# A gated-recurrence plus MLP kernel: new start order, decay rows on ScalarE's DMA ring, and q/k turned by the transposing DMA

## The chip, the cores and the metric

The kernel runs on 1 core of one Trainium2 chip. The metric is the device time of one execution in microseconds (us). The kernel before takes 344.27 us (median of 3 runs, 342.91 to 344.88). The span of a profile is about 2 us below the device time of the same run.

Engines: PE is TensorE's matmul side, PEld its weight loads, DVE is VectorE, ACT is ScalarE, POOL is GpSimd, SP is SyncE. A name with q at the end (ACTq, SPq) is that engine's sequencer, issuing a DMA. An engine's ring is the queue through which the DMAs that it issues go. A DMA has landed when its data is written; times to landing are counted from the start of its issue.

## The reference

```python
# attention, per batch and head, D = 48, S = 768; 4 batches, 8 heads
scale = min(|a|, 0.999) / (|a| + 1e-6);  a_n = a * scale        # a = a_re + i a_im
S_t = a_n[t, :, None] * S_{t-1} + k[t, :, None] * v[t, None, :]    # complex state 48 x 48
y[t] = q[t] @ Re(S_t)
# MLP on x = y, as 3072 tokens of 384, hidden 1536
h = gelu(x @ w_gate) * (x @ w_val)
out = x + sigmoid(x @ w_res) * (h @ w_out)
```

## The kernel before

The recurrence is done in chunks. A group `g` is 256 time steps of one batch (2 chunks of 128, three groups to a batch, 12 groups). Two groups are a unit; there are 6 units. A unit has a gating part and an attention part, and its tokens then go through the MLP:

- Gating: logarithm and angle of `a`, cumulative sums over time by a matmul with a triangular matrix, then Exp (`E`, `Ei`) and Sin (`CS`). All of it ends in products `Q` and `K` with 96 columns a head.
- Attention: each head's Q and K are turned (transposed), `at` = KT x QT, masked to `atm`, times `v`, plus the carried state `Gb`; `dk` updates the state.
- MLP: 12 steps of gate (`gp`) and value (`vp`) matmuls, 6 matmuls a step, then `op`.

The program alternates a gating phase (`phase_x`) and an MLP phase (`phase_y`). In the MLP phase of unit u, the first half of the attention of unit u+1 is woven between the gate/value matmuls; in the following gating phase the rest of it. In the trace ScalarE loads another function table (1.28 us each) at each change of phase, which marks the phases.

A group that is not the first of its batch (groups 1, 2, 4, 5, ...) needs its decay factors with the head dimension on the partitions. The kernel writes rows of 384 numbers to DRAM and reads them back turned:

```python
def turn(nm, g, srcs):                       # called for lm (m1), then for E and Ei (m2)
    md = dr.tile([n, DM], FP, ...)           # a scratch in DRAM
    for i, src in enumerate(srcs):
        nc.gpsimd.dma_start(out=md[i:i + 1, :], in_=src)
    m = mp.tile([128, n, H], FP, ...)
    for u in range(2):                       # 4-byte pieces
        nc.gpsimd.dma_start(out=m[u * D:(u + 1) * D]..., in_=md.rearrange("r (h d) -> d (r h)", h=H))
```

Q and K are turned by TensorE, four heads at a time, with a copy out of PSUM:

```python
def a():
    tp = psT.tile([128, 1024], BF, ...)
    ... # 4 nc.tensor.transpose of Q, 4 of K
    qk = sqp.tile([128, 1024], BF, ...)
    nc.scalar.copy(out=qk[0:DD, 0:512], in_=tp[0:DD, 0:512])
    nc.vector.tensor_copy(out=qk[0:DD, 512:1024], in_=tp[0:DD, 512:1024])
    ... # 4 matmuls at = K^T x Q^T, then atm = at * mask
...
def hi(f):                                   # each attention step is recorded like this
    with tc.high_priority():                 # the scheduler puts it as early as its inputs allow
        f()
```

## Time and profile before

The busy shares of the kernel before, in 40 slices of its 341.4 us (each digit is a tenth; PEclk is the granted clock of TensorE):

```profile
PE 267.3 (78%) x2054; PEld 160.6 (47%) x2080; DVE 245.4 (72%) x440; ACT 203.0 (59%) x338; POOL 67.1 (20%) x104
...
PE   0330544298689979899897999779999989999995
...
PEclk9996585559699999999999999999999999999999
DMA  9999999999999999527422620021000210002002
```

DMA is full in the first 16 slices (137 us). In the first 8 (68 us) TensorE is at most half busy; from slice 12 on (94 us) it is nearly full and at full clock.

The chain of work that ended last, within those first 95 us of the kernel before (start us, us, what):

```profile
21.80 6.91 DMA dm_219<-ar
...
44.80 13.88 DMA dm_266<-ar
...
76.31 8.40 DMA dm_663<-Ei
...
85.89 4.42 DMA m_666<-dm_663
```

These are decay rows of 1.5 KB, and their turned copies. So in this chain the start is held mostly by tiny transfers on a full DMA: with two more turned copies of 5.6 and 4.6 us they make up 44 of the 94 us, and the longest piece for an input, a load of `v`, is 8.4 us.

The table of phases used from here on is read from ScalarE's timeline: "start" ends where the gelu table of unit 0 is loaded, an MLP phase goes from a gelu table to the next log/exp table (the last one, which has no following unit, from gelu table to gelu table), a gating phase from there to the next gelu table, and "tail" is the rest of the span. Phases are read to 0.1 us, so that sums can be off by 0.1.

| kernel before | us |
|---|---|
| start | 94.0 |
| five MLP phases | 26.0, 26.4, 26.6, 25.5, 26.0: sum 130.5 |
| four gating phases | 20.8, 20.1, 20.7, 18.5: sum 80.1 |
| tail | 36.9 |

Busy time in the MLP phases of the kernel before, by windows (window, length, busy of PE, PEld, DVE, ACT, POOL with the number of instructions, granted clock, DMA share, GB/s; the sum is over all five. A DMA packet counts in the window in which it starts, so a share can exceed 1):

```profile
187.20:213.80 26.60, 26.05 (x269) 16.75 (x271) 24.31 (x44) 16.79 (x31) 0.00 (x0) 1.00 0.28 53
...
sum 130.50, PE 127.12 PEld 80.69 DVE 116.13 ACT 82.42 POOL 9.01; mean PE 25.42 PEld 16.14 DVE 23.23 ACT 16.48 POOL 1.80
```

TensorE is busy in 127.1 of 130.5 us, VectorE in 116.1.

### The profile page before, as it was taken

What the parts mean: (1) busy time and instruction counts of PE and PEld (TensorE: products, weight loads), DVE (VectorE), ACT (ScalarE), POOL (GpSimd) and SP (SyncE); (2) the same over time, 40 slices, a digit from 0 to 9 for tenths busy, and PEclk for the clock granted to TensorE, in tenths of its full rate; (3) what the DMA queues carried; (4) which work ended last, traced back from release to release, by engine and by line L of the source; (5) the groups of instructions that cost most, each with busy time, mean ns of one, the idle gap of its engine ahead of it and who ended that gap; (6) DMA issues with size and microseconds to landing.
All of it is one profiled execution on the core that took longest, in us unless ns stands there. A gap on an engine that the chain in (4) does not pass through costs nothing.

```text
span 341.4 us, 5552 instructions
## 1 busy us (share of the span) xinstructions
PE 267.3 (78%) x2054; PEld 160.6 (47%) x2080; DVE 245.4 (72%) x440; ACT 203.0 (59%) x338; POOL 67.1 (20%) x104
## 2 busy tenths in 40 slices
PE   0330544298689979899897999779999989999995
PEld 0110224275256545465554566445665556565452
DVE  1322696249999649999389998499994799855443
ACT  3365434349665696756896656977568275662530
POOL 9423710050522224102232000150001300000000
PEclk9996585559699999999999999999999999999999
DMA  9999999999999999527422620021000210002002
GB/s 139 136 139 175 176 184 196 175 170 171 155 167 162 169 133 172 109 46 72 25 63 54 118 46 2 2 48 47 3 2 1 50 46 2 0 2 92 2 1 92
DMA packets 135258, 30.25 MB, mean 89 GB/s; under 512 B 127168, under 2 KB 135232, under 8 KB 135232
## 3 DMA queue, kind: packets, MB, share of 16 engines
q1 hardware_dynamic: 103296, 23.60, 40.6%
q0 software_dynamic: 31936, 6.31, 21.9%
q8 instruction: 16, 0.26, 0.3%
q14 instruction: 10, 0.08, 0.1%
HBM read 31.33 MB, written 4.76 MB: 106 GB/s over the span
## 4 chain that ended last, share of the span: by engine, by line
PE 47%; DMA 18%; DVE 15%; ACT 9%; issue 7%; POOL 3%; ACTq 0%; DVEq 0%; POOLq 0%
PE vp L414 12%; PE gp L410 11%; PE op L434 6%; DMA dm_266<-ar 4%; DMA v<-in_v_dram 4%; PE tp L320 3%; PE at L327 3%; PE tp L317 3%; PE rp L426 3%; DMA dm_663<-Ei 2%; ACT L445 2%; DVE fg L237 2%; DVE r L234 2%; DMA dm_219<-ar 2%; ACT CS L119 2%
## 5 line engine op out<-in xcount | busy, mean ns | idle before, releaser
L410 PE MATMUL gp<-xT,wg 128*128 128x512 bf16 x196 | 61.5, 382 | 7.6 <-DVE xT L401 4.6
L414 PE MATMUL vp<-xT,wv 128*128 128x512 bf16 x210 | 60.3, 382 | 0.3
L322 ACT COPY qk<-tp 96x512 bf16<-96x512 bf16 x48 | 27.9, 581 | 28.3 <-PE tp L320 15.1
L180 DVE TENSOR_TENSOR ai<-s,ai 128x768 f32<-128x768 f32 x12 | 11.1, 955 | 38.5 <-ACT s L119 26.9
L330 DVE TENSOR_TENSOR atm<-at,mask_81 128x512 bf16<-128x512 f32 x48 | 32.8, 683 | 7.2 <-PE at L327 7.2
L410 PEld LDWEIGHTS <-wg 128*128 128x128 bf16 x216 | 20.0, 98 | 23.0 <-issue 8.9
L317 PE MATMUL tp<-ident,Q 128*96 128x128 bf16 x192 | 20.1, 231 | 13.4 <-DVE qk L323 8.6
L142 POOL DMA_DIRECT2D v<-in_v_dram x24 | 21.3, 902 | 43.0 <-PE y L367 22.4
L414 PEld LDWEIGHTS <-wv 128*128 128x128 bf16 x216 | 20.4, 98 | 19.3 <-issue 0.8
L317 PEld LDWEIGHTS <-Q 128*96 128x96 bf16 x192 | 17.3, 131 | 21.4 <-issue 10.0
L323 DVE COPY qk<-tp 96x512 bf16<-96x512 bf16 x48 | 19.9, 414 | 10.1 <-ACT qk L322 9.6
L203 PE MATMUL csl<-ar,lt0a 128*128 128x384 f32 x24 | 12.3, 601 | 18.6 <-DVE ar L189 18.5
L119 ACT ACTIVATE CS<-fg,hpi 128x768 bf16<-128x768 f32 x12 | 11.2, 935 | 24.1 <-DVE fg L237 24.1
L445 ACT ACT_TABLE_LOAD x18 | 23.1, 1283 | 1.0 <-PEq L547 0.7
L320 PE MATMUL tp<-ident,K 128*96 128x128 bf16 x192 | 22.1, 235 | 0.0
L227 PE MATMUL cst<-ai,lt0b 128*128 128x384 f32 x24 | 11.6, 568 | 13.4 <-ACT ai L119 13.1
L327 PE MATMUL at<-qk 96*128 96x128 bf16 x192 | 20.4, 228 | 0.1
L437 DVE SCALAR_TENSOR_TENSOR ot<-sg,op 128x384 f32<-128x384 f32 x24 | 13.2, 549 | 9.4 <-PE op L434 9.4
L365 PE MATMUL y<-v,atm 128*128 128x48 bf16 x192 | 17.9, 187 | 2.5 <-DVE atm L330 2.4
L365 PEld LDWEIGHTS <-atm 128*128 128x128 bf16 x192 | 13.5, 98 | 12.8 <-DVE atm L330 11.6
L320 PEld LDWEIGHTS <-K 128*96 128x96 bf16 x192 | 17.3, 133 | 0.0
L357 PEld LDWEIGHTS <-K 128*96 128x96 bf16 x160 | 13.3, 138 | 6.5 <-DVE K L292 4.2
(155 smaller groups left out, 626.3 us busy)
## 6 DMA issues: line engine op xcount, KB each, us to landing
ar<-in_a_re_dram SPq DMA_DIRECT2D x24, 192.0 KB, 5.7
ai<-in_a_im_dram SPq DMA_DIRECT2D x24, 192.0 KB, 5.5
q<-in_q_dram SPq DMA_DIRECT2D x24, 192.0 KB, 5.1
k<-in_k_dram SPq DMA_DIRECT2D x24, 192.0 KB, 5.0
out_dram<-ot SPq DMA_DIRECT2D x24, 192.0 KB, 1.9
v<-in_v_dram POOLq DMA_DIRECT2D x24, 96.0 KB, 6.3
wg<-in_moe_w_gate_dram POOLq DMA_DIRECT2D x4, 288.0 KB, 9.2
wv<-in_moe_w_val_dram POOLq DMA_DIRECT2D x4, 288.0 KB, 10.5
```

The costliest lines, as they stand in the source:

```text
L142: nc.gpsimd.dma_start(out=t[:, c], in_=rows(v, g, c))
L317: nc.tensor.transpose(out=tp[0:DD, j * 128:j * 128 + 128], in_=Q(x), identity=ident)
L320: nc.tensor.transpose(out=tp[0:DD, 512 + j * 128:640 + j * 128], in_=K(x), identity=ident)
L322: nc.scalar.copy(out=qk[0:DD, 0:512], in_=tp[0:DD, 0:512])
L323: nc.vector.tensor_copy(out=qk[0:DD, 512:1024], in_=tp[0:DD, 512:1024])
L327: nc.tensor.matmul(out=at[:, j], lhsT=qk[0:DD, 512 + j * 128:640 + j * 128], rhs=qk[0:DD, j * 128:j * 128 + 128], start=True, stop=True)
L330: nc.vector.tensor_tensor(out=atm, in0=at, in1=mask4, op=OP.mult)
L365: nc.tensor.matmul(out=ys, lhsT=st["atm", hg][:, j], rhs=V(h), start=True, stop=first)
L410: nc.tensor.matmul(out=gp, lhsT=wg[:, fi, ffi * 128:(ffi + 1) * 128], rhs=xT[:, fi, :], start=(fi == 0), stop=(fi == KD - 1))
L414: nc.tensor.matmul(out=vp, lhsT=wv[:, fi, ffi * 128:(ffi + 1) * 128], rhs=xT[:, fi, :], start=(fi == 0), stop=(fi == KD - 1))
L434: nc.tensor.matmul(out=ps, lhsT=h2[:, ffi, jj * 128:(jj + 1) * 128], rhs=wo[:, ffi, :], start=(ffi == 0), stop=(ffi == KF - 1))
L445: tab(nc.scalar.preload_act_table_set(nm))
```

## The change

The intent: (1) start unit 0 sooner, by loading its inputs first and gating it alone; (2) take the decay rows off GpSimd's ring, where they stand behind weight loads, and put them on ScalarE's; (3) take the Q/K transposes of units 1 to 5 from TensorE, and their PSUM copies from ScalarE and VectorE, and let SyncE's transposing DMA do them; (4) issue the stores on GpSimd. The diff, cut to its core:

```diff
+    PE_TURNED = 2
-    lda bufs=6, ldq bufs=4
+    lda bufs=5, ldq bufs=3;  pF bufs=1 (for fg alone);  pT bufs=3 (for QT and KT)
-    psT = ... bufs=1 ...;  psA = ... bufs=1
+    psA = ... bufs=2
...
+    def decay_rows(g):
+        er = pS.tile([1, DM], FP, tag="r", name="er")
+        act(out=er, in_=T["lm", g][0:1, 0:DM], func=AF.Exp)
+        md = dr.tile([3, DM], FP, tag="md", name="md")
+        for i, src in enumerate((T["E", g - 1][127:128, DM:W], T["Ei", g][0:1, 0:DM], er)):
+            nc.scalar.dma_start(out=md[i:i + 1, :], in_=src)
+    def decay(g):
+        m = mp.tile([128, 3, H], FP, tag="m", name="m")
+        for u in range(2):
+            nc.scalar.dma_start(out=m[u * D:(u + 1) * D]..., in_=T["md", g]...)
+        ... # M = product of the three rows, on GpSimd (was VectorE)
...
     # products: Q and K are written into 128 columns a head, the last 32 zero
+                if g >= PE_TURNED:
+                    for c in range(C):
+                        tt = pT.tile([128, H, 128], BF, tag=nm + "T", name=nm + "T")
+                        nc.sync.dma_start_transpose(out=tt, in_=t[:, c * H:(c + 1) * H]...)
...
-        nc.sync.dma_start(out=out[t0:t0 + 128, :], in_=ot)
+        nc.gpsimd.dma_start(out=out[t0:t0 + 128, :], in_=ot)
...
-    for g in gs(0) + gs(1):
-        load_a(g)
-    for g in gs(0):
-        load_q(g)                     # q, k and v
-    after_landing(T["k", 0], load_w_in)
+    for g in gs(0):
+        load_a(g)
+    for g in gs(0):
+        load_q(g); load_v(g)
+    for g in gs(1):
+        load_a(g)
+    after_landing(T["ai", 2], load_w_in)
+    for g in gs(1):
+        load_q(g)
     # phase_x(-1) gates unit 0 alone; phase_x(0) gates unit 1 and starts unit 2
+            after_landing(T["q", 2], lambda: [load_v(g) for g in gs(1)])
+            after_landing(T["q", 3], load_w_out)
```

More of the change, by code (lines that the diff above doesn't have):

```diff
@@ L85 @@
     wr = singles.tile([128, KD, DM], BF, name="wr")
-    lda = ctx.enter_context(tc.tile_pool(name="lda", bufs=6))
-    ldq = ctx.enter_context(tc.tile_pool(name="ldq", bufs=4))
+    lda = ctx.enter_context(tc.tile_pool(name="lda", bufs=5))
+    ldq = ctx.enter_context(tc.tile_pool(name="ldq", bufs=3))
     ldv = ctx.enter_context(tc.tile_pool(name="ldv", bufs=6))
@@ L92 @@
     pE = ctx.enter_context(tc.tile_pool(name="pE", bufs=2))
+    pF = ctx.enter_context(tc.tile_pool(name="pF", bufs=1))
     pQ = ctx.enter_context(tc.tile_pool(name="pQ", bufs=2))
     pK = ctx.enter_context(tc.tile_pool(name="pK", bufs=1))
+    pT = ctx.enter_context(tc.tile_pool(name="pT", bufs=3))
     sqp = ctx.enter_context(tc.tile_pool(name="sqp", bufs=2))
@@ L103 @@
     psM = ctx.enter_context(tc.tile_pool(name="psM", bufs=4, space=PSUM))
-    psT = ctx.enter_context(tc.tile_pool(name="psT", bufs=1, space=PSUM))
-    psA = ctx.enter_context(tc.tile_pool(name="psA", bufs=1, space=PSUM))
+    psA = ctx.enter_context(tc.tile_pool(name="psA", bufs=2, space=PSUM))
     psY = ctx.enter_context(tc.tile_pool(name="psY", bufs=1, space=PSUM))
     psD = ctx.enter_context(tc.tile_pool(name="psD", bufs=1, space=PSUM))
+    Qb = [singles.tile([128, C * H, 128], BF, name="Qb%d" % i) for i in range(2)]
+    Kb = [singles.tile([128, C * H, 128], BF, name="Kb%d" % i) for i in range(2)]
+    for t in Qb + Kb:
+        nc.gpsimd.memset(t[:, :, DD:128], 0.0)
     T = {}
@@ L139, in load_q, with load_v @@
             T[nm, g] = t
+    def load_v(g):
         t = ldv.tile([128, C, H, D], BF, tag="v", name="v")
@@ L223, in cs_t @@
         if c == 0:
-            T["fg", g] = pE.tile([128, C * H, 2, D], FP, tag="fg", name="fg")
+            T["fg", g] = pF.tile([128, C * H, 2, D], FP, tag="fg", name="fg")
         sl = slice(c * DM, (c + 1) * DM)
@@ L245, in p2_sin @@
         act(out=T["CS", g][:, :, 1], in_=T["fg", g][:, :, 1], func=AF.Sin, scale=2.0 * math.pi)
-    def turn(nm, g, srcs):
-        n = len(srcs)
-        md = dr.tile([n, DM], FP, tag="d" + nm, name="d" + nm)
-        for i, src in enumerate(srcs):
-            nc.gpsimd.dma_start(out=md[i:i + 1, :], in_=src)
-        m = mp.tile([128, n, H], FP, tag=nm, name=nm)
-        for u in range(2):
-            nc.gpsimd.dma_start(out=m[u * D:(u + 1) * D].rearrange("p r h -> p (r h)"),
-                                in_=md.rearrange("r (h d) -> d (r h)", h=H))
-        T[nm, g] = m
-    def decay0(g):
-        turn("m1", g, [T["lm", g][0:1, 0:DM]])
-    def decay1(g):
-        m = T["m1", g]
-        act(out=m[0:DD], in_=m[0:DD], func=AF.Exp)
-    def decay2(g):
-        turn("m2", g, [T["E", g - 1][127:128, DM:W], T["Ei", g][0:1, 0:DM]])
-    def decay3(g):
-        m = T["m2", g]
+    def decay_rows(g):
[4 more added lines that the diff above has]
+            nc.scalar.dma_start(out=md[i:i + 1, :], in_=src)
+        T["md", g] = md
+    def decay(g):
+        m = mp.tile([128, 3, H], FP, tag="m", name="m")
+        for u in range(2):
+            nc.scalar.dma_start(out=m[u * D:(u + 1) * D].rearrange("p r h -> p (r h)"),
+                                in_=T["md", g].rearrange("r (h d) -> d (r h)", h=H))
         M = mp.tile([128, H], FP, tag="M", name="M")
-        nc.vector.tensor_tensor(out=M[0:DD], in0=m[0:DD, 0], in1=m[0:DD, 1], op=OP.mult)
-        nc.vector.tensor_tensor(out=M[0:DD], in0=M[0:DD], in1=T["m1", g][0:DD, 0], op=OP.mult)
+        nc.gpsimd.tensor_tensor(out=M[0:DD], in0=m[0:DD, 0], in1=m[0:DD, 1], op=OP.mult)
+        nc.gpsimd.tensor_tensor(out=M[0:DD], in0=M[0:DD], in1=m[0:DD, 2], op=OP.mult)
         T["M", g] = M
@@ L289, in x @@
             def x():
-                t = pQ.tile([128, C * H, 2, D], BF, tag=nm, name=nm)
+                t = (Qb if nm == "Q" else Kb)[g % 2]
                 sb = T[src, g].rearrange("p (x u d) -> p x u d", u=1, d=D).to_broadcast([128, C * H, 2, D])
-                nc.vector.tensor_tensor(out=t, in0=T["CS", g], in1=sb, op=OP.mult)
+                nc.vector.tensor_tensor(out=t[:, :, 0:DD].rearrange("p x (u d) -> p x u d", u=2), in0=T["CS", g],
+                                        in1=sb, op=OP.mult)
                 T[nm, g] = t
+                if g >= PE_TURNED:
+                    for c in range(C):
+                        tt = pT.tile([128, H, 128], BF, tag=nm + "T", name=nm + "T")
+                        nc.sync.dma_start_transpose(out=tt, in_=t[:, c * H:(c + 1) * H].rearrange("p x e -> p (x e)"))
+                        T[nm + "T", g, c] = tt
             return x
@@ L301, in attention, with pe_transposes @@
         st = {}
-        def Q(x):
-            return T["Q", g][:, x].rearrange("p u d -> p (u d)")
-        def K(x):
-            return T["K", g][:, x].rearrange("p u d -> p (u d)")
         def V(h):
             return T["v", g][:, c, h]
+        def pe_transposes(hg):
+            if hg == 0:
+                for nm in ("Q", "K"):
+                    T[nm + "T", g, c] = pT.tile([128, H, 128], BF, tag=nm + "T", name=nm + "T")
+            tp = psM.tile([128, 2, 4, 128], BF, tag="mm", name="tp")
+            for i, nm in enumerate(("Q", "K")):
+                for j in range(4):
+                    nc.tensor.transpose(out=tp[0:DD, i, j], in_=T[nm, g][:, c * H + hg * 4 + j, 0:DD], identity=ident)
+            hs = slice(hg * 4, hg * 4 + 4)
+            nc.scalar.copy(out=T["QT", g, c][0:DD, hs], in_=tp[0:DD, 0])
+            nc.vector.tensor_copy(out=T["KT", g, c][0:DD, hs], in_=tp[0:DD, 1])
         def grp(hg):
             def a():
-                tp = psT.tile([128, 1024], BF, tag="tp", name="tp")
-                for j in range(4):
-                    x = c * H + hg * 4 + j
-                    nc.tensor.transpose(out=tp[0:DD, j * 128:j * 128 + 128], in_=Q(x), identity=ident)
-                for j in range(4):
-                    x = c * H + hg * 4 + j
-                    nc.tensor.transpose(out=tp[0:DD, 512 + j * 128:640 + j * 128], in_=K(x), identity=ident)
-                qk = sqp.tile([128, 1024], BF, tag="qk", name="qk")
-                nc.scalar.copy(out=qk[0:DD, 0:512], in_=tp[0:DD, 0:512])
-                nc.vector.tensor_copy(out=qk[0:DD, 512:1024], in_=tp[0:DD, 512:1024])
-                st["qk", hg] = qk
+                if g < PE_TURNED:
+                    pe_transposes(hg)
+                QT, KT = T["QT", g, c], T["KT", g, c]
                 at = psA.tile([128, 4, 128], FP, tag="at", name="at")
                 for j in range(4):
-                    nc.tensor.matmul(out=at[:, j], lhsT=qk[0:DD, 512 + j * 128:640 + j * 128],
-                                     rhs=qk[0:DD, j * 128:j * 128 + 128], start=True, stop=True)
+                    nc.tensor.matmul(out=at[:, j], lhsT=KT[0:DD, hg * 4 + j], rhs=QT[0:DD, hg * 4 + j],
+                                     start=True, stop=True)
                 atm = sqp.tile([128, 4, 128], BF, tag="atm", name="atm")
@@ L356, in dk @@
             for h in range(H):
-                nc.tensor.matmul(out=d[0:DD, h * D:(h + 1) * D], lhsT=K(c * H + h), rhs=V(h),
+                nc.tensor.matmul(out=d[0:DD, h * D:(h + 1) * D], lhsT=T["K", g][:, c * H + h, 0:DD], rhs=V(h),
                                  start=(c == 0 and h == 0), stop=(h == H - 1), skip_group_check=True)
@@ L366, in yy @@
                 if not first:
-                    nc.tensor.matmul(out=ys, lhsT=st["qk", hg][0:DD, j * 128:j * 128 + 128],
+                    nc.tensor.matmul(out=ys, lhsT=T["QT", g, c][0:DD, h],
                                      rhs=T["Gbf"][0:DD, h], start=False, stop=True)
@@ L472, in phase_x @@
         d1 = [g for g in g1 if g % NS > 0]
-        d2 = [g for g in g2 if g % NS > 0]
         ops = [call(op_step, u - 1, jj) for jj in range(4)] if 0 <= u - 1 < NU else []
@@ L484, in ex @@
             pend.pop(0)()
-        def p1(g):
-            return p1_steps(g) + ([call(decay0, g)] if g % NS > 0 else [])
         csls = [call(csl, g, c) for g in g1 for c in range(C)]
-        exs = [ex for _ in g1 for _ in range(C)]
-        dec = [call(decay2, g) for g in d1]
-        atn = [table("trig_and_small")] + [call(p1_arctan, g) for g in g2]
+        exs = [ex for _ in g1 for _ in range(C)] + [call(decay_rows, g) for g in d1]
+        dec = [call(decay, g) for g in d1]
         cst = [call(carry, g) for g in g1] + [call(cs_t, g, c) for g in g1 for c in range(C)]
         sin = [call(p2_sin, g) for g in g1]
-        dec1 = [call(decay1, g) for g in d1]
-        dec3 = [call(decay3, g) for g in d1]
+        trig = table("trig_and_small")
         table("natural_log_exp_and_others")()
         if u < 0:
-            for f in [st for g in g1 for st in p1(g)] + csls + exs + dec + zip_steps([p1(g) for g in g2]) + dec1:
-                f()
-            for f in atn[:1] + [call(p1_arctan, g) for g in g1] + cst + sin + atn[1:] + dec3:
+            for f in ([st for g in g1 for st in p1_steps(g)] + csls + exs + [trig]
+                      + [call(p1_arctan, g) for g in g1] + dec + cst + sin):
                 f()
             return
-        weave((0.0, 0.12, csls), (0.05, 0.5, zip_steps([p1(g) for g in g2])), (0.01, 0.01, dec1), (0.12, 0.45, exs),
-              (0.46, 0.46, dec), (0.2, 0.65, cst), (0.7, 0.95, atn + sin), (0.95, 0.95, dec3), (0.0, 0.8, att), (0.1, 1.0, ops))
+        atn = [call(p1_arctan, g) for g in g2]
+        p1 = zip_steps([p1_steps(g) for g in g2])
+        if u == 0:
+            first = [st for g in g1 for st in p1_steps(g)]
+            weave((0.0, 0.3, first), (0.3, 0.4, csls), (0.4, 0.6, exs), (0.4, 0.7, p1),
+                  (0.7, 0.75, [trig] + [call(p1_arctan, g) for g in g1]), (0.72, 0.72, dec), (0.75, 0.9, cst),
+                  (0.9, 1.0, sin + atn), (0.0, 0.8, att))
+            return
+        weave((0.0, 0.12, csls), (0.05, 0.5, p1), (0.12, 0.45, exs), (0.46, 0.46, dec), (0.2, 0.65, cst),
+              (0.7, 0.95, [trig] + atn + sin), (0.0, 0.8, att), (0.1, 1.0, ops))
     def phase_y(u):
@@ L520 @@
         load_q(g)
-    after_landing(T["k", 0], load_w_in)
+        load_v(g)
+    for g in gs(1):
[3 more added lines that the diff above has]
+        load_q(g)
     for u in range(-1, NU + 1):
@@ L526 @@
         if u == -1:
-            for g in gs(1):
-                load_q(g)
-            after_landing(T["k", 2], load_w_out)
+            after_landing(T["q", 2], lambda: [load_v(g) for g in gs(1)])
+            after_landing(T["q", 3], load_w_out)
         phase_y(u)
@@ L532 @@
             load_q(g)
+            load_v(g)
 _INS = ['q', 'k', 'v', 'a_re', 'a_im', 'moe_w_gate', 'moe_w_val', 'moe_w_out', 'moe_w_res']
```

## The prediction

> **What bounds the kernel before.** Two stretches, by the busy-time table over windows and the timelines.
>
> Start, 0 to 94 us (where unit 0's MLP begins): DMA is above 90% busy, yet ScalarE and TensorE wait more for tiny transfers than for data. The chain of waits holds 13.9 us for one decay row (dm_266<-ar), 8.4 for dm_663<-Ei, 6.9 for dm_219, and 4.4 to 5.6 for each turned copy: they sit in GpSimd's ring behind the weight loads. ScalarE stood idle from 55.4 to 64.3 us for m_268. With DMA idle such rows landed in 1.6 us.
>
> Steady state, about 46.5 us per unit: an MLP/attention phase of 26.5 us (PE busy 26, DVE 24, ACT 17), in which the chain is TensorE almost without a gap, and a gating phase of 20 us (ACT 16.9, DVE 15.4, PE 16), a chain of ACT, DVE `fg`, ACT Sin.
>
> **What the change does.**
> 1. Start: unit 0's inputs come first and its gate runs alone; rows go through ScalarE's ring. Unit 0's attention should start near 35 us instead of 50. Then ScalarE must do two units' gating (13.4 us of Ln/Exp/Square, 3.9 Exp, 3.3 Arctan, 3.5 Sin, 7.5 copies), and unit 2's a arrives near 65 us at the measured 1.4 to 1.8 us a load. MLP 0 starts near 76 us instead of 94: -18 us.
> 2. Units 1 to 5 lose 64 TensorE transposes each (3.7 us in the chain), 8 ACT copies of 0.58 and 8 DVE copies of 0.41 us, all in the TensorE-bound phase. DVE is then nearly as long, so 3.3 us of 26.5: -16 us over five phases.
> 3. Added: 40 DMA transposes of 256 KB. [...] TensorE has four gate/value pairs (5 us) to cover them.
> 4. `fg` has one buffer: group 2's `fg` (two 0.55, one 0.95 us) now waits for group 1's Sin. About +2 us in each of four gating phases: +9 us with ScalarE's own DMA issues (about 0.4 us each, 5 per decaying group).
> 5. Stores by GpSimd: +1 us at the tail, else free.
>
> Sum: 344.3 - 18 - 16 + 9 + 1 = 320 us.
>
> **Prediction: 320 us, 8 in 10 between 300 and 340. Faster by over 2%: 0.82; within 2%: 0.11; slower: 0.07.**
>
> **What would show it.** (1) The gelu table load of unit 0 at about 76 us; no decay row over 4 us on the chain. (2) The MLP phases (gelu table load to next log/exp table load) at 23 us, DVE above 90% in them. (3) Transposes landing in 2 to 4 us, and few TensorE waits on KT or QT. (4) Gating phases of 21 to 22 us, ScalarE idle before the second pair of Sin. (5) TensorE busy 30 to 35 us less in total.
>
> **What would make it wrong.** [...] at 3 us each, four in sequence, TensorE would wait for KT twice per unit and give back the 16 us; at 5 us or more SyncE's ring becomes the bound, loads behind it come late, and the kernel is slower. [...] If the start is bound by DMA bytes, not waits, -18 shrinks to -8. On the other side, if the gating phases shorten too, 305.

The sum: step 3 adds nothing to it (344.3 - 18 - 16 + 9 + 1 = 320.3 us). The -16 us of step 2 supposes that the transposes land within step 3's 5 us of cover; that was the author's estimate.

## The result

The changed kernel takes 369.14 us (median, 366.80 to 371.04); the kernel before took 343.59 us in the same rounds. The ratio is 1.074, 95% interval 1.066 to 1.082. A ratio here is the mean time of one kernel's fast runs over that of the other's fast runs of the same rounds, so it is not quite the ratio of the medians. The prediction of 320 us, 300 to 340, is wrong, in sign too. All outputs are right.

The busy shares after, in 40 slices of 368.1 us:

```profile
PE 264.5 (72%) x1738; PEld 149.7 (41%) x1760; DVE 232.2 (63%) x384; ACT 185.7 (50%) x298; POOL 52.2 (14%) x93
...
PE   0356665040839798587889789887799987999993
...
PEclk9988556555787899969999989999899998999999
DMA  9999999999969743949965497042860226612002
```

All engines do less work, and the span grew by 26.7 us. TensorE shed 316 instructions but only 2.8 us of busy time, and its clock is not full in the middle of the run any more.

| phase | before | after | difference | predicted |
|---|---|---|---|---|
| start | 94.0 | 107.6 | +13.6 | -18 |
| five MLP phases | 130.5 | 131.6 | +1.1 | -16 |
| four gating phases | 80.1 | 90.3 | +10.2 | +9 |
| tail | 36.9 | 38.7 | +1.8 | +1 |

**The start.** The chain of work of the changed kernel, up to the first transposes:

```profile
60.54 13.55 DMA ar<-in_a_re_dram
...
84.49 2.40 DMA k<-in_k_dram
...
89.77 5.10 DMA m<-md
...
106.35 3.24 DMA KT<-Kb_154
```

ScalarE's timeline in the same stretch (start us, us, what, and in brackets the idle time before it and what ended it):

```profile
74.17 0.84 ACT L128 ACTIVATE ar<-ar 128x768 f32<-128x768 f32 x1 [12.11 <-DMA ar<-in_a_re_dram]
...
84.60 0.22 ACTq L265 DMA_DIRECT2D md<-er  x1
84.94 0.84 ACT L128 ACTIVATE s<-ai 128x768 f32<-128x768 f32 x1 [2.72 <-DMA k<-in_k_dram]
...
99.94 0.93 ACT L128 ACTIVATE CS<-fg,hpi 128x768 bf16<-128x768 f32 x1 [7.50 <-DVE fg L248]
...
104.43 0.94 ACT L128 ACTIVATE CS<-fg,hpi 128x768 bf16<-128x768 f32 x1 [2.82 <-DVE fg L248]
...
107.58 1.28 ACT L450 ACT_TABLE_LOAD   x1
```

ScalarE waits 12.1 us for unit 2's `a`. It then stands for 2.7 us before it may issue the row `md<-er`: what it waits for is a load of `k`, which that row doesn't use. In this trace the DMAs of SyncE and ScalarE take turns on eight completion counters (semaphores 101 to 104 and 106 to 109). In all 168 cases in which a counter is used again, the next DMA is issued after the last one's final update, in 11 of them within 0.15 us of it; this is how a row comes to wait for a load. The row takes counter 102, which a load of `k`, issued by SyncE at 78.83 us, filled at 84.52 us; the row goes out at 84.60. Then `m<-md` takes 5.1 us to land. `M` is made from it, and in VectorE's timeline `fg` comes after the `G` that uses `M`:

```profile
95.51 0.55 DVE L349 TENSOR_TENSOR G<-G,M 96x384 f32<-96x384 f32 x1 [2.62 <-POOL M L275]
```

ScalarE's Sin waits 7.5 us for `fg`; in 2.6 of these VectorE itself stands still for `M`, in the other 4.9 it works.

**The MLP phases.** Windows over the five MLP phases of the changed kernel, columns as before:

```profile
256.90:283.70 26.80, 23.58 (x197) 13.02 (x199) 20.08 (x32) 12.57 (x23) 0.54 (x1) 0.94 0.51 87
...
sum 131.50, PE 114.90 PEld 65.31 DVE 94.51 ACT 62.19 POOL 8.18; mean PE 22.98 PEld 13.06 DVE 18.90 ACT 12.44 POOL 1.64
```

VectorE lost 21.6 us of work, ScalarE 20.2, TensorE 12.2. Yet the phases lost nothing: TensorE stood idle for 16.6 us (131.5 - 114.9; before it was 3.4). The transposes into tile KT of the changed kernel (duration min/median/max in ns, then first and last start), and TensorE's waits for KT over the whole run (us, times, longest):

```profile
L299 SPq DMA_TRANSPOSE KT<-Kb_154 x10: 1261/1308/2762, 106.4 to 306.6; - x10
```

```profile
PE at L332 <- DMA KT<-Kb_154: 9.2, 4, 3.8
PE at L332 <- DMA KT<-Kb_155: 4.8, 4, 2.7
PE at L332 <- DVE KT L323: 2.2, 2, 1.6
```

The transposes take 1.3 us each just to issue, and TensorE waited 16.2 us for turned K: 14.0 for the transposing DMA, and 2.2 in the start for VectorE's copies of unit 0, which TensorE turns. One such wait, by the timelines of SyncE and of TensorE in the MLP phase that begins at 256.9 us:

```profile
256.87 2.61 SPq L299 DMA_TRANSPOSE QT<-Qb_152  x2
259.57 4.12 SPq L299 DMA_TRANSPOSE KT<-Kb_154  x2
```

```profile
261.01 0.81 PE L419 MATMUL vp<-xT,wv 128*128 128x512 bf16 x3
264.36 0.76 PE L332 MATMUL at<-QT,KT 96*128 96x128 bf16 x8 [2.54 <-DMA KT<-Kb_154]
264.91 1.49 PE L415 MATMUL gp<-xT,wg 128*128 128x512 bf16 x3
```

And the windows around it (the granted clock is the number after POOL's):

```profile
260.00:262.00 2.00, 1.78 (x8) 0.53 (x6) 1.34 (x4) 0.91 (x2) 0.00 (x0) 1.00 1.25 83
262.00:264.30 2.30, 0.00 (x0) 0.00 (x0) 0.61 (x1) 0.00 (x0) 0.00 (x0) 1.00 1.05 226
264.30:266.00 1.70, 1.64 (x11) 1.01 (x12) 0.95 (x2) 0.00 (x0) 0.00 (x0) 0.62 0.44 82
266.00:268.00 2.00, 2.00 (x15) 1.20 (x15) 1.21 (x3) 0.60 (x1) 0.00 (x0) 0.50 0.00 0
```

Four transposes go out one after another (Q's two, then K's two), and the first use of them stands 7.5 us after the first issue. TensorE's fixed order gives it only some three and a half gate/value steps before that use, so it idles for 2.5 us. Then the clock is 0.50: three `gp` matmuls take 1.49 us, where three `vp` matmuls of the same shape took 0.81 before. In the clock records of this run the half clock lasts 3.4 us after this wait (264.7 to 268.1 us), and 20.5 us in total over the five MLP phases. TensorE was busy in 17.7 of these; half of that, about 9 us, is an estimate of what the lower clock cost.

**The gating phases** are 28.8, 22.0, 21.4 and 18.1 us; 8 of the 10 added us are in the first one, unit 2's. There ScalarE stands 3.3 and 1.8 us while it issues `m<-md`, and then 5.4 us for `fg`, while VectorE waits 2.4 us for `M` and 2.9 us for `op` matmuls at half clock. The single `fg` buffer shows in the timeline above: VectorE stands 1.3 us for the first pair of Sin, within the 2.82 us that ScalarE waits. But the kernel before, with two buffers, has a wait of 2.12 us at the same place, so the buffer's share there is below the predicted 2 us.

Two theories were set up. *Latency*: the transposes, and the rows, are held by latency and by order (a ring, a shared counter, a fixed place in TensorE's program), not by bytes. The rival, *bytes and work*: DMA is too full for 40 more transfers of 256 KB, or the new order of work is itself longer.

### The profile page after: what moved, and what is told of

Read it like the earlier page. It is cut to its first block, busy times and chain, and to the rows that moved or that the text cites. A ratio compares the mean times of both kernels' runs of the same rounds, so it can differ in the third digit from the quotient of the medians.

```text
span 368.1 us, 4840 instructions
## 1 busy us (share of the span) xinstructions
PE 264.5 (72%) x1738; PEld 149.7 (41%) x1760; DVE 232.2 (63%) x384; ACT 185.7 (50%) x298; POOL 52.2 (14%) x93
## 4 chain that ended last, share of the span: by engine, by line
DMA 25%; PE 23%; issue 21%; DVE 16%; ACT 8%; SPq 2%; POOL 2%; ACTq 1%; POOLq 0%; DVEq 0%
DMA k<-in_k_dram 7%; PE vp L419 6%; DMA m<-md 5%; PE gp L415 5%; DMA KT<-Kb_155 4%; DMA ar<-in_a_re_dram 4%; DMA KT<-Kb_154 3%; PE at L332 3%; PE csl L214 2%; PE op L439 2%; ACT L450 2%; DMA ai<-in_a_im_dram 2%; DVE fg L248 2%; PE rp L431 2%; DVE r L245 2%
## 5 line engine op out<-in xcount | busy, mean ns | idle before, releaser
L419 PE MATMUL vp<-xT,wv 128*128 128x512 bf16 x210 | 63.0, 395 | 0.7 <-issue 0.4
L445 POOL DMA_DIRECT2D out_dram<-ot x24 | 13.2, 550 | 172.6 <-DVE ot L443 172.0
L153 POOL DMA_DIRECT2D v<-in_v_dram x24 | 21.4, 895 | 82.3 <-PE y L372 71.5
L332 PE MATMUL at<-QT,KT 96*128 96x128 bf16 x192 | 21.0, 248 | 16.6 <-DMA KT<-Kb_154 9.2
L128 ACT ACTIVATE CS<-fg,hpi 128x768 bf16<-128x768 f32 x12 | 11.2, 933 | 31.6 <-DVE fg L248 31.5
L332 PEld LDWEIGHTS <-KT 96*128 96x128 bf16 x192 | 15.6, 112 | 22.9 <-DMA KT<-Kb_154 10.8
L281 DVE TENSOR_TENSOR qE<-q,E 128x768 bf16<-128x768 f32 x12 | 11.4, 953 | 21.1 <-ACT E L128 21.1
L375 ACT CAST x<-y 128x384 bf16<-128x384 f32 x24 | 11.5, 478 | 20.9 <-PE y L372 17.4
L442 DVE SCALAR_TENSOR_TENSOR ot<-sg,op 128x384 f32<-128x384 f32 x24 | 13.2, 550 | 13.7 <-PE op L439 13.6
L370 PE MATMUL y<-v,atm 128*128 128x48 bf16 x192 | 19.8, 195 | 2.0 <-DVE atm L335 1.8
L128 ACT ACTIVATE ar<-ar 128x768 f32<-128x768 f32 x12 | 9.8, 839 | 19.6 <-DMA ar<-in_a_re_dram 19.5
L128 ACT ACTIVATE sg<-rp 128x384 f32<-128x384 f32 x24 | 11.8, 492 | 9.7 <-PE rp L431 9.7
L199 DVE SCALAR_TENSOR_TENSOR ar<-s,ar 128x768 f32<-128x768 f32 x12 | 11.3, 952 | 7.8 <-ACT s L128 7.8
```

What stands on the lines that cost most here:

```text
L128: tab(nc.scalar.activation(**kw))
L153: nc.gpsimd.dma_start(out=t[:, c], in_=rows(v, g, c))
L332: nc.tensor.matmul(out=at[:, j], lhsT=KT[0:DD, hg * 4 + j], rhs=QT[0:DD, hg * 4 + j], start=True, stop=True)
L370: nc.tensor.matmul(out=ys, lhsT=st["atm", hg][:, j], rhs=V(h), start=True, stop=first)
L419: nc.tensor.matmul(out=vp, lhsT=wv[:, fi, ffi * 128:(ffi + 1) * 128], rhs=xT[:, fi, :], start=(fi == 0), stop=(fi == KD - 1))
L442: nc.vector.scalar_tensor_tensor(out=ot, in0=T["sg", u][:, jj], scalar=1.0, in1=ps, op0=OP.add, op1=OP.mult)
```

## The experiments

18 kernels were run. Names that begin with `b_` or `x` are edits of the kernel before, the others of the kernel after. Every run had three rounds beside the kernel before, whose medians were 343.3 to 345.2 us. The phases, in us, from each profile:

| kernel | time | ratio, 95% interval | start | MLP | gating | tail |
|---|---|---|---|---|---|---|
| before | 344.3 | 1 | 94.0 | 130.5 | 80.1 | 36.9 |
| after | 369.1 | 1.074, 1.066 to 1.082 | 107.6 | 131.6 | 90.3 | 38.7 |
| pe_all | 377.1 | 1.100, 1.093 to 1.108 | 109.2 | 116.9 | 104.4 | 43.3 |
| old_start | 360.2 | 1.050, 1.042 to 1.059 | 99.1 | 126.8 | 91.9 | 38.9 |
| rows_pool | 372.5 | 1.087, 1.079 to 1.094 | 104.9 | 138.7 | 89.0 | 38.5 |
| b_rows_act | 357.6 | 1.043, 1.036 to 1.049 | 103.5 | 135.0 | 82.0 | 37.4 |
| b_rows_sp | 348.1 | 1.012, 1.007 to 1.016 | 99.8 | 132.0 | 77.6 | 37.4 |
| b_wlate | 340.0 | 0.987, 0.981 to 0.993 | 83.5 | 132.7 | 86.2 | 36.9 |
| b_turn | 365.6 | 1.063, 1.059 to 1.068 | 93.6 | 146.0 | 88.5 | 36.9 |
| pt4 | 370.1 | 1.075, 1.068 to 1.082 | 106.9 | 128.8 | 91.6 | 38.8 |
| a_first | 369.6 | 1.071, 1.064 to 1.078 | 106.5 | 133.0 | 91.7 | 38.8 |
| att_nohi | 350.4 | 1.015, 1.008 to 1.022 | 108.1 | 107.0 | 90.7 | 41.6 |
| b_stores_pool | 348.2 | 1.008, 1.002 to 1.014 | 94.2 | 131.0 | 81.1 | 40.0 |
| b_wlate_st | 342.5 | 0.989, 0.981 to 0.998 | 86.4 | 136.0 | 79.7 | 39.8 |
| first_pool | 372.1 | 1.079, 1.073 to 1.086 | 104.7 | 137.9 | 89.0 | 38.3 |
| b_nohi | 342.1 | 0.995, 0.990 to 0.999 | 94.5 | 113.7 | 90.0 | 42.2 |
| b_turn_nohi | 333.8 | 0.970, 0.966 to 0.975 | 94.4 | 107.6 | 90.0 | 40.1 |
| x1 | 333.2 | 0.970, 0.965 to 0.976 | 85.2 | 119.9 | 88.9 | 40.2 |
| x2 | 326.2 | 0.948, 0.942 to 0.954 | 85.4 | 109.0 | 89.9 | 39.8 |
| first_late | 373.7 | 1.086, 1.080 to 1.091 | 91.7 | 152.0 | 90.6 | 38.7 |

### One part of the change at a time

**pe_all**: the kernel after with all groups turned on TensorE.

```diff
-    PE_TURNED = 2
+    PE_TURNED = NG
```

> The changed kernel with all q/k transposes on TensorE again (the constant PE_TURNED set to all groups). Theory A: the transposing DMA neither gained nor lost, because TensorE's waits for KT (about 16 us in the changed kernel) took back what it saved; then the MLP phases go back to about 26 us each without waits on KT, the start stays at 105 to 108 us, and the total stays at 364 to 372 us. Theory B: the transposing DMAs, or the loads held behind them in SyncE's ring, are what made the kernel slower; then the total falls to 342 to 352 us.

Measured: 377.1 us, slower than the kernel after and outside both theories. The MLP phases fell by 14.7 us to 116.9, but the gating phases grew by 14.1 and the tail by 4.6. This is not a clean undoing: the PSUM bank of the old transposes is gone, so here they take the buffers of the gate and value matmuls. Work has moved between the phases too (116.9 us is less than the 130.5 of the kernel before, which turns on TensorE as well), so this run decides nothing about the transposes.

**b_turn**: the kernel before with the transposing DMA, its tiles and its buffer counts, and nothing else of the change.

```diff
+    (from the kernel after: PE_TURNED = 2, Qb/Kb, pT, pF, psA bufs=2, lda bufs=5, ldq bufs=3,
+     nc.sync.dma_start_transpose for g >= PE_TURNED)
```

> The kernel before with only the transposing DMA for units 1 to 5, and the smaller buffers that it needs (a 5, q and k 3, fg 1). Theory A (the transposes gain about as much as setting all of them back cost, 8 us, less what fg's single buffer takes): start as before, MLP phases 24 to 26 us, gating phases 21 to 23 us, total 336 to 346 us. Theory B (transposes and loads in one ring hurt each other): MLP phases 27 us or more, total 350 us or more.

Measured: 365.6 us. This part alone costs 6.3%: +15.5 us in the MLP phases, +8.4 in the gating phases, nothing in the start or the tail. Unit 0's MLP phase alone takes 39.8 us instead of 26.0. SyncE's timeline around the gelu load of that phase (93.6 us):

```profile
93.86 3.31 SPq L138 DMA_DIRECT2D ai<-in_a_im_dram  x2
97.21 0.95 SPq L138 DMA_DIRECT2D ar<-in_a_re_dram  x1
98.27 3.54 SPq L305 DMA_TRANSPOSE QT<-Qb  x2
```

Unit 1's first transpose goes out at 98.3 us, although VectorE had its `Qb` ready at 91.0 us: loads of later units stand before it in the same ring, as the lines show. The smaller buffers were not run by themselves; b_turn_nohi below has the same ones and is faster than the kernel before, so they are not the main loss.

**b_rows_act** and **b_rows_sp**: the kernel before with only the decay rows and turned copies on another ring.

```diff
-            nc.gpsimd.dma_start(out=md[i:i + 1, :], in_=src)
+            nc.scalar.dma_start(out=md[i:i + 1, :], in_=src)        # b_rows_sp: nc.sync
-            nc.gpsimd.dma_start(out=m[u * D:(u + 1) * D]...
+            nc.scalar.dma_start(out=m[u * D:(u + 1) * D]...         # b_rows_sp: nc.sync
```

> The kernel before with only the decay rows' DMAs moved to ScalarE's ring. Theory A (the rows behind the weight loads cost the start about 17 us; on ScalarE's ring they land at once): gelu table load of unit 0 at 78 to 86 us instead of 94, later gating phases 1 to 3 us longer, total 330 to 340 us. Theory B (ScalarE is then held by the waits for landing and for shared slots, in program order): total 342 us or more.

> The kernel before with only the decay rows' DMAs moved, this time to SyncE's ring. [...] the waits for a free counter and for the rows to land are now SyncE's. Theory A (on ScalarE's ring the loss was ScalarE standing in program order in those waits): ScalarE's waits of 10.7 us for the turned copies in the start go, gelu table load of unit 0 at 84 to 96 us, total 334 to 348 us. Theory B (it is the rows behind the loads in any hardware ring, or the loads behind them, whoever waits): total 352 us or more.

The "shared slots", here and below in old_start, are the completion counters of the kernel after's trace, where a row went out at 84.60 us, after a load of `k` had filled its counter at 84.52.

Measured: +4.3% on ScalarE's ring (its theory B), +1.2% on SyncE's (348.1 us: the edge of its theory A, whose start, 99.8 us, came later than said). The start is 9.5 and 5.8 us longer. Two lines of b_rows_act, from the chain of work and from ScalarE's timeline:

```profile
68.47 8.69 DMA q<-in_q_dram
77.17 0.24 ACTq L253
```

```profile
93.31 0.48 ACT L399 COPY xT<-tpx 128x384 bf16<-128x384 bf16 x1 [10.68 <-DMA m<-dm]
```

The row at 77.17 us went out only when a load of `q`, which it doesn't read, had landed, 8.7 us after that load's own issue, and ScalarE stood 2.2 us for it. Later the copy of `xT` stood for 10.7 us in ScalarE's program. The profile names a turned copy there; that copy was issued only at 90.02 us, and ScalarE's work before it had ended at 82.6. What held the issue is not shown by the lines; that it was a load's counter, as in the kernel after, is the author's reading. What is new is that the engine issuing the rows has other work, which waits with them.

**old_start**: the kernel after with the old order of loads, and units 0 and 1 gated together in the first phase.

```diff
-    (loads of a(0), q/k/v(0), a(1), weights, q/k(1); phase_x(-1) gates unit 0 alone)
+    (loads of a(0), a(1), q/k/v(0), weights, later q/k(1); phase_x(-1) gates units 0 and 1)
```

> The changed kernel with units 0 and 1 gated together and unit 1's and 2's a loaded early, as before. Theory A (the start lost its time because ScalarE, in program order, waits for unit 2's a, which the new load order brings late on a saturated DMA): the gelu table load of unit 0 comes at 88 to 97 us instead of 107.6, total 352 to 360 us. Theory B (it was ScalarE's own ring, the decay rows and shared completion slots): the gelu load stays at 103 us or later and the total at 364 us or more.

Measured: 360.2 us, against 369.1 of the kernel after: the new order of the start costs 8.5 of the 13.6 us that the start lost (which part of it, the loads or the gating, was not separated). The result lies between the two theories. The remaining 5.1 are there with the old order too, with the rows on ScalarE's ring.

**rows_pool**: the kernel after with the rows back on GpSimd's ring.

```diff
-            nc.scalar.dma_start(out=md[i:i + 1, :], in_=src)
+            nc.gpsimd.dma_start(out=md[i:i + 1, :], in_=src)       (and the turned copies)
```

> The changed kernel with the decay rows and their turned copies on GpSimd's ring again. Theory A (in program order on ScalarE, five DMA issues per decaying group and the wait for the rows to land hold up the gating phase, 8 us in that of unit 2): gating phase of unit 2 falls from 28.8 to 21 to 24 us; the rows may be late behind the weights in the start, up to 8 us; total 358 to 368 us. Theory B (GpSimd's ring was the real trouble and ScalarE's ring is a gain everywhere): total 372 us or more.

Measured: 372.5 us. The start is 2.7 us shorter and the MLP phases are 7 us longer; ScalarE stands 20.3 us before unit 1's Sin, in one piece. So in the new order the rows cost as much on GpSimd's ring, where the loads of `v` and of the weights go too.

**b_stores_pool**: the kernel before with the stores on GpSimd.

```diff
-        nc.sync.dma_start(out=out[t0:t0 + 128, :], in_=ot)
+        nc.gpsimd.dma_start(out=out[t0:t0 + 128, :], in_=ot)
```

> The kernel before with only the stores moved to GpSimd's ring. Theory A (stores are off the chain; SyncE is idle then): within 2 us of before, 342 to 346 us, tail about 1 us longer. Theory B (SyncE held loads back behind stores that wait for DVE): 336 to 341 us.

Measured: +0.8%; the tail is 40.0 us instead of 36.9 and all else within a microsecond. A small cost, at the tail alone.

### The MLP phases: buffers, or latency against a fixed order

**pt4**: the kernel after with four buffers for QT and KT instead of three, in case a transpose waits for a buffer.

```diff
-    pT = ctx.enter_context(tc.tile_pool(name="pT", bufs=3))
+    pT = ctx.enter_context(tc.tile_pool(name="pT", bufs=4))
```

> The changed kernel with four buffers for each of QT and KT in place of three. Theory A (the second wait for KT in each MLP phase, 3.5 to 6.8 us, comes from SyncE: the transpose of q's second half waits for a buffer that TensorE frees late, and KT's stand behind it in the ring): waits on the second group's KT fall below 2 us, MLP phases at 23 to 25 us, total 357 to 364 us. Theory B (the wait is the transposes' own time, 1.3 us of issue each and about 3.3 us from the last issue to landing): nothing changes by more than 4 us.

Measured: 370.1 us, no gain (the ratios overlap). A wait for a free buffer is not what holds TensorE; that theory fell.

**att_nohi**: the kernel after, where the attention steps of the DMA-turned groups lose their high priority. The scheduler then places them later between the gate/value matmuls of the same program.

```diff
-                with tc.high_priority():
-                    f()
+                if g < PE_TURNED:
+                    with tc.high_priority():
+                        f()
+                else:
+                    f()
```

> The changed kernel with the attention steps of the DMA-turned units at ordinary scheduling priority, so that TensorE's program has at least five gate/value pairs ahead of the first product that reads KT, in place of about three and a half, and the second group follows later. Theory A (the transposes' saving was lost to TensorE waiting for KT[...]): TensorE's waits on KT fall from about 16 us to under 4 us, clock 1.0 in the MLP phases, total 352 to 362 us. Theory B (the loss in these phases is elsewhere, in DVE or the completion counters): total 365 us or more.

Measured: 350.4 us, 19 us less than the kernel after. Start and gating phases are as there (108.1, 90.7); the MLP phases fell from 131.6 to 107.0 us, the tail grew by 2.9. TensorE's line among the waits on KT, and the sum of the MLP windows, of att_nohi:

```profile
  PE at L332: 6.6, 4
```

```profile
sum 107.00, PE 101.33 PEld 53.05 DVE 80.69 ACT 58.42 POOL 5.05; mean PE 20.27 PEld 10.61 DVE 16.14 ACT 11.68 POOL 1.01
```

TensorE's wait fell from 16.2 to 6.6 us over the run (the part for the transposing DMA from 14.0 to 4.3), and its idle time in the MLP phases from 16.6 to 5.7. The transposes are the same, with the same bytes; only the place of their first use moved. That decides for latency against a fixed order, and against bytes. Some attention work also moved into the gating phases (TensorE's busy time in the MLP phases is 13.6 us lower), which is why a control is needed.

**b_nohi**: that control, the kernel before with the same lines (high priority for g < 2 only), transposes still on TensorE. **b_turn_nohi**: b_turn with the same lines.

> The kernel before, transposes on TensorE, with only the priority of the attention steps of units 1 to 5 lowered, as att_nohi had it (which took 19 us off the changed kernel). It is the control of att_nohi. Theory A (att_nohi gained by giving the transposing DMAs time to land): here nothing waits for them, and the gain is small, total 338 to 346 us. Theory B (the other order of attention is better in itself): total 320 to 334 us.

> The kernel before with the transposing DMA and its buffers (as b_turn, 365.6 us) and the lower priority of attention. Theory A (b_turn's loss in the MLP phases was TensorE's waits for KT; the transposes themselves are worth about 3.7 us a phase): MLP phases at 20 to 23 us, except the first, total 326 to 340 us. Theory B (in this kernel the transposes stand behind loads in SyncE's ring): first MLP phase still 30 us or more, total 345 us or more.

Measured, on the same chip in the same rounds: b_nohi 342.1 us, b_turn_nohi 333.8 us. In the kernel before the later placing is worth only 0.5%: it moves 17 us out of the MLP phases, 10 into the gating phases and 5 into the tail. With the DMA transposes it turns a loss of 6.3% into a gain of 3.0%. The last two kernels differ in who turns Q and K and in the tiles and buffers that go with it, and the difference, 8.3 us, is what the transposing DMA is worth here once its latency is nearly covered (TensorE still waits 2.0 us for KT): 6.1 us in the MLP phases and 2.1 in the tail.

### The start: whose wait is it?

**b_wlate**: the kernel before, where the weight loads leave GpSimd's ring until unit 1's rows are through it.

```diff
-    after_landing(T["k", 0], load_w_in)
...
-            after_landing(T["k", 2], load_w_out)
+            after_turn(T["m1", 2], load_w_in)      # after group 2's first turned copy has landed
+        if u == 0:
+            after_turn(T["m2", 2], load_w_out)     # after its second
```

> The kernel before with only two gates changed: the loads of the input weights start after unit 1's decay row is turned, those of the output weights after the next turned copy has landed, so that no row stands behind a weight load in GpSimd's ring. Theory A (the rows' waits of 13.9 and 8.4 us were on the chain): ScalarE's idle 8.9 us for m_268 and the 8.4 us for dm_663<-Ei shrink to about 3 us each, gelu load at 80 to 88 us, total 329 to 338 us. Theory B (the start is bound by DMA bytes, and weights or unit 2's data come later in turn): total 341 us or more.

Measured: 340.0 us, 1.3% faster than before. The start fell from 94.0 to 83.5 us, which shows that the weight loads held the rows, in the ring or on the full DMA (this run can't tell which); 8 us were given back later (gating +6.1, MLP +2.2). Bytes moved with them: in unit 2's gating phase DMA now carries 176 GB/s for 25.6 us, before 156 for 20.8. A row still takes 9.3 us and a turned copy 4.1 us in its chain, so the ring was not the whole of it.

**b_wlate_st**: b_wlate with the stores on GpSimd, as a candidate.

> The kernel before with the weight loads after the turned rows (as b_wlate, 340.0 us) and the stores on GpSimd's ring. In b_wlate the gating phase of unit 2 took 25.5 us, with 4.9 us of waiting for a store that stood in SyncE's ring behind the loads. Theory A (that wait goes when the store has another ring): that phase at 21 to 23 us, total 334 to 338 us. Theory B (the DMA engines are full then, whatever the ring): 339 us or more.

Measured: 342.5 us, no better than b_wlate (340.0); the intervals overlap.

**a_first**: the kernel after, where unit 2's `a` is asked for before unit 1's q and k, to take away the 12.1 us wait for `ar`.

```diff
     after_landing(T["ai", 2], load_w_in)
-    for g in gs(1):
-        load_q(g)
     for u in range(-1, NU + 1):
...
         if u == -1:
+            for g in gs(1):
+                load_q(g)
```

> The changed kernel with one pair of lines in the load order swapped: unit 2's a is asked for before unit 1's q and k. Theory A (ScalarE, in program order, stands 4.5 and 12.1 us in the first gating phase after unit 0's because unit 2's a arrives at 60 and 74 us on a saturated DMA): those waits fall under 8 us together, gelu table load of unit 0 at 96 to 103 us, total 357 to 364 us. Theory B (the start is bound by the sum of bytes that must have landed, weights included, so the order among them only moves the wait): gelu load at 105 us or later, total 365 us or more.

Measured: 369.6 us, no gain. The wait for `ar` went, and in its place ScalarE stood 11.9 us in issuing two rows (they went out at 70.12 and 76.75 us); the profile names the landing of a load of `k` as the end of that wait. The 12.1 us were thus not the cause, only the first wait in line.

**first_pool**: a_first with the rows on GpSimd's ring as well (a_first and rows_pool together).

> The changed kernel with unit 2's a asked for before unit 1's q and k (as a_first) and the decay rows on GpSimd's ring (as rows_pool). Each alone left the gelu table load of unit 0 at 105 to 107 us; in a_first ScalarE's 16.6 us of waiting for a were gone, but it then stood 11.9 us for a k load's completion counter and 8.2 us more before the turned rows. Theory A (the wait moved to the counters that ScalarE's ring shares with SyncE's): with both edits it goes, gelu load at 88 to 98 us, total 350 to 362 us. Theory B (all loads and weights together set the time on a full DMA): gelu load at 103 us or later, total 365 us or more.

Measured: 372.1 us. Its chain of work, and ScalarE's timeline:

```profile
59.98 13.46 DMA v<-in_v_dram
...
74.00 11.59 DMA md<-er
...
86.78 5.16 DMA m<-md
```

```profile
97.01 0.94 ACT L128 ACTIVATE CS<-fg,hpi 128x768 bf16<-128x768 f32 x1 [24.03 <-DVE fg L248]
```

Now both former waits are gone, and the row itself takes 11.6 us behind unit 1's `v`. ScalarE has nothing to do for 24 us, and in 19.2 of these VectorE stands still for `M`.

**first_late**: first_pool, with everything else of GpSimd's ring (v of units 1 and 2, the output weights) asked for only after unit 1's turned rows have landed.

```diff
-            after_landing(T["q", 2], lambda: [load_v(g) for g in gs(1)])
-            after_landing(T["q", 3], load_w_out)
+        if u == 0:
+            after_turn(T["mt", 2], lambda: [load_v(g) for g in gs(1)] + [load_w_out()]
+                                           + [load_v(g) for g in gs(2)])
```

> The kernel after with unit 2's a asked for before unit 1's q and k, the rows on GpSimd's ring, and everything else of that ring (unit 1's v, the output weights, unit 2's v) asked for only after unit 1's turned rows have landed. Theory (the first 107 us are set by the decay rows' round trip through a ring and a DMA that are full): the rows land in 3 to 4 us each and unit 0's gelu load comes at 92 us or earlier. Rival (the order of work, unit 0 alone and unit 1's gating after it, is what costs; or the bytes): the wait moves to another load, and gelu stays at 103 us or later. The total is not expected to beat the kernel before in either case: the MLP phases are those of the kernel after.

Measured: 373.7 us, and the start is 91.7 us, 13.0 less than in first_pool. The rows set the start: the theory held, at the edge of its number. Since the big loads left both the ring and the DMA, this doesn't tell which of the two had held the rows. ScalarE's timeline of first_late, VectorE's, SyncE's, and TensorE's:

```profile
84.04 0.94 ACT L128 ACTIVATE CS<-fg,hpi 128x768 bf16<-128x768 f32 x1 [11.83 <-DVE fg L254]
...
91.68 1.28 ACT L457 ACT_TABLE_LOAD   x1
```

```profile
79.60 0.55 DVE L356 TENSOR_TENSOR G<-G,M 96x384 f32<-96x384 f32 x1 [6.94 <-POOL M L282]
```

```profile
87.66 5.52 SPq L306 DMA_TRANSPOSE QT<-Qb  x2
```

```profile
102.34 1.03 PE L339 MATMUL at<-QT,KT 96*128 96x128 bf16 x8 [12.38 <-DMA KT<-Kb]
```

Even with an emptied ring the round trip (a row 4.2 us, the turned copy 5.9, on a DMA that is 90% busy or more) still costs: ScalarE waits 11.8 us, in 6.9 of which VectorE stands still for `M`. And the 16 us that the start won over the kernel after were lost at once. The earlier MLP phase meets the postponed loads, the transposes need 5.5 us a pair instead of 2.6, and TensorE waits 12.4 us for KT: the first MLP phase takes 41.1 us.

### Versions that beat both kernels

**x1**: b_wlate's late weights, the DMA transposes and the later placing, stores on SyncE, rows on GpSimd, old order of the start. **x2**: x1 with unit 1 turned on TensorE as well, so that the first transposing DMA comes later (K's first is issued at 138.5 us, in x1 at 100.9).

```diff
-    PE_TURNED = 2         # x1
+    PE_TURNED = 4         # x2
-                if g < 2:
+                if g < 2:     # unchanged: high priority for unit 0 only
```

> A candidate from the parts that gained: the kernel before, rows on GpSimd's ring with the weight loads after them (b_wlate), the transposing DMA for units 1 to 5, attention of these at ordinary priority, stores on SyncE. Expected if the gains add: b_wlate's 4 us and 10 to 15 us from the transposes, total 318 to 332 us. If the transposes of unit 1 stand behind loads on a DMA that is full until about 125 us: 335 us or more.

> The kernel before with late weights, DMA transposes (now from unit 2 on only, unit 1 turned on TensorE) and without high priority for the attention of the units that the DMA turns. Theory (the first MLP phase of x1, 34.7 us, is long because unit 1's transposes stand behind loads in SyncE's ring while DMA is full): unit 0's MLP phase falls to 23 to 26 us, the rest stays, total 322 to 328 us. Rival (that phase is long for another reason, such as unit 1's late inputs or weights): the phase stays over 30 us and the total at 331 to 336 us.

Measured: x1 333.2 us, x2 326.2 us (324.37 to 327.42), 5.2% faster than the kernel before. In x1 the start fell to 85.2 us, but unit 0's MLP phase took 34.7 us: its transposes again stood behind loads (SyncE issues loads of `a` from 80.99 to 95.4 us, and the first transpose at 95.59). In x2 that phase takes 23.5 us, as its theory said. From the instructions on tile KT of x2, TensorE's waits and the landing time of the 16 KT transposes:

```profile
  PE at L344: 2.1, 1
...
DMA to landing us min/median/max: 3.0/3.2/4.8
```

TensorE waits 2.1 us for KT in the whole run instead of 16.2. Against the kernel before, the start gives 8.6 us, the MLP phases 21.5; the gating phases take back 9.8 and the tail 2.9.

## Why the prediction was wrong, point by point

- **What bounds the kernel before** was read rightly: b_wlate shortened the start by 10.5 us only by taking the weight loads out of the rows' way, and TensorE is busy in 127.1 of the 130.5 us of the MLP phases.
- **Step 1, "MLP 0 starts near 76 us instead of 94: -18 us", failed.** It came at 107.6 us. Unit 0's gating did end about as predicted (its table load is at 36.6 us instead of 54.1, its first `at` product at 41.3 instead of 53.3), but the step summed ScalarE's work and left out the round trip of unit 1's rows, though it had just named that wait as the bound before. It assumed that ScalarE's ring would be free of it. There the rows wait on the completion of unrelated loads and hold ScalarE meanwhile (2.7 us for one row in the kernel after): moving the rows alone cost 14 us in b_rows_act (4.3%), 9.5 of them in the start. The prediction named this risk, and gave it no weight. With the rows' ring emptied (first_late) the start is 91.7 us; take away the 6.9 us for which VectorE still stands for `M` and it would be about 85, an estimate, 9 more than the predicted 76. So the wait for the rows is the larger part of what was missing, 23 of 31.6 us; the rest stays open, and part of it is VectorE's own work before `fg`, 4.9 us of ScalarE's wait, which a sum of ScalarE's work leaves out.
- **Step 2, "-16 us over five phases", failed: +1.** The work went as said and more (ScalarE -20, VectorE -22, TensorE -12 us busy), so the mechanism is right. TensorE's waits for the transposing DMA (14.0 us, of which 12.3 in the MLP phases) and about 9 us (estimate) of half clock took its place. In b_turn_nohi against b_nohi the transposes are worth 8 us, half of the 16.
- **Step 3, that 5 us of cover are enough for the transposes, failed**, and it is what sank step 2. The cost that the prediction took for one of them, no run had measured. In the kernel after, issue alone takes 1.3 us each, in series, about 200 GB/s (256 KB in 1.3 us), and even in x2 one lands 3.2 us after its issue begins. Four in series would be 3 x 1.3 + 3.2 = 7.1 us and are 7.5 in the window shown, against 5 us of cover. The prediction's warning, "at 3 us each, four in sequence, TensorE would wait for KT twice per unit and give back the 16 us", describes what came, although each takes 1.3 and not 3 us to issue; the half clock after the wait is what it didn't see.
- **Step 4, "+9 us" in the gating phases: +10.2, but not for its reasons alone.** b_turn has +8.4 of it without ScalarE's rows, and b_rows_act +1.9 with nothing but them. 8 us sit in unit 2's phase, where the trace shows ScalarE's DMA issues and the wait for `M`. The share of the single `fg` buffer was not run by itself and stays open; by the trace of the start it is below the 2 us a phase that were predicted.
- **Step 5, "+1 us at the tail, else free"**: 1.8 us; alone, in b_stores_pool, 3.1.
- **"What would show it"** (5), TensorE busy 30 to 35 us less, was wrong by ten times: 2.8 us. Busy time includes the matmuls that run at half clock: by the clock records TensorE was busy at half clock for 22.7 us before and 53.9 us after, and half of the difference, about 16 us, is an estimate of what that hid.

What stays open: whether the ring or the full DMA holds the rows; how much of the gating phases' growth is the `fg` buffer and how much is attention work that the other placing moves there; and how the start of first_late would go on a DMA that is not full, since the bytes have to be moved at some time.

## What to carry to other kernels

A DMA that replaces on-chip work has a latency as well as a rate (here 1.3 us of issue each and, in x2, 3.2 us from there to landing): count the issues in series and the landing, and compare with what the consumer's fixed program order puts before the first use; then move the use, not only the producer. A wait of TensorE can cost more than itself: in the kernel after, after one of 2.54 us the clock was half for 3.4 us, though after one of 2.17 us in the same run (at 247.3 us) it stayed full. Moving a tiny transfer to another ring didn't shorten its wait here (b_rows_act: 8.7 us from a load's issue until the row could go out, on a DMA over 90% busy; +4.3% in all), and it put the wait into an engine that had work to do; take the big loads out of its way instead (b_wlate: start 94.0 to 83.5 us), and look at which phase then has to carry them.
